# Top-32 attention, gate and phase mixer on one core: the threshold of each tile from one MAX8 with eight added columns

## The chip, the cores and the metric

The kernel runs on one core of a Trainium2 chip. The metric is device time in microseconds, the median of the runs taken; lower is better. Engines are named as in the profile: PE is TensorE (matmuls; PEld its weight loads), DVE is VectorE, ACT is ScalarE, POOL is GpSimd, SP is the queue that issues most DMAs.

## What is computed

Three stages in float32, for 4 batches, 8 heads, 576 tokens, 64 columns a head:

```python
scores = (q @ k.T) / sqrt(64)
kth = the 32nd largest score of each row
scores = where(scores >= kth, scores, -1e9)
attn = exp(scores - max); attn = attn / (sum(attn) + 1e-9)
x = attn @ v
gate = sigmoid(sum over 5 taps of conv_w[k] * x[t + k - 4])
x = (gate * (x @ w_val)) @ w_out
theta = x @ w_theta
u = x + w_tok_r @ (x * cos(theta)) + w_tok_i @ (x * sin(theta))
out = u + max(u @ w_ch, 0)
```

The change touches the second line alone, the search for the 32nd largest score of a row, and the scale in which the scores are kept for it.

## The kernel before

The 4 x 8 x 576 rows of scores are cut into 144 tiles of 128 rows and 576 columns. A loop over steps runs all engines through a software pipeline: in step i, tile i gets its first search and older tiles get their later stages. What a step does, and in which order, stands in a list of names (`STEP`, and `SOON` for the first half of the tiles). The instructions of VectorE and ScalarE stand in exactly that order; TensorE, GpSimd and the DMA queues are ordered by the scheduler by priority, which follows the order of the program.

What happens to tile i, with the lines:

- `scores_pe`, `scores_out` (L536, L550): TensorE makes the scores in PSUM, ScalarE copies them to SBUF with the factor 0.125 as tile `s`.
- `pick` (L565), step i: VectorE takes MAX8 (the eight largest, sorted) of each of six stretches of 96 columns, 48 candidates. Interleaved with this, the candidates of tile i - 1 are sorted by three MAX8 and two MATCH_REPLACE8: the 24 largest of them, `tops`.
- `count` (L581): ScalarE takes the sign of (24th candidate - score), +1 for scores below, -1 for the others, as `n`, and sums the signs in `acc`. A row with c scores not below has acc = 576 - 2c.
- `below` (L589), step i + 2: GpSimd makes y = s * n. Scores below keep their value, those above turn negative. Tile y has one buffer, so the next y waits for `rest`.
- `rest` (L596), step i + 3: VectorE takes MAX8 of y, the eight largest scores below the 24th candidate.
- `nmax` (L603): GpSimd negates the largest and the 24th of three tiles, for the exponent's bias and for the check.
- `select` (L605), once for a group of three tiles: c is 24 if the candidates held all of the 24 largest, and more if a stretch had over eight of them. Three VectorE operations pick the (32 - c)th of the eight: compare `counts` with `acc` (L611), multiply with the eight (L613), sum over eight (L614). They go into the list `apart`, from which `mask_between` (L1247) takes one at a time, three in a step: one ahead of the mask and two behind it. The operations of the list `fill` (the conversion of weights, L328, L329, L324, up to 300 us) are taken in the same places.
- `expo` (L645): ScalarE takes exp(s - max).
- `mask` (L650), step i + 6: VectorE makes (s >= threshold) * exp and its sum in one operation (L656).
- `turn`, `close`: TensorE transposes the masked tile and multiplies by v; VectorE, ScalarE and GpSimd divide by the sums (L700, L701, L767) and make the gate (L792 to L804).

The dense stages (`front`, `back`) are cut into pieces that TensorE does between the steps; the last of them follow after the tiles. `check` (L631) runs once behind the last tile: if a threshold is not above a tiny bound, or a 24th candidate isn't positive, a flag makes the whole program run again in a safe form (`safe`), which searches directly.

Of the kernel before, what the change touches and what calls it, by code (L numbers as in the profile page):

```python
# [11 lines left out]
F32 = mybir.dt.float32  # L12
# [4 lines left out]
AF = mybir.ActivationFunctionType  # L17
ALU = mybir.AluOpType
# [58 lines left out]
@with_exitstack  # L77
def attention_gate_phase_mixer(ctx, tc, *tensors):


    nc = tc.nc
    keep = ctx.enter_context(tc.tile_pool(name="keep", bufs=1))
    flag = keep.tile([1, 1], F32, name="flag")
    mixer(tc, *tensors, flag)

    over = nc.values_load(flag.bitcast(I32), min_val=0, max_val=0x7F000000,
                          skip_runtime_bounds_check_because="a count of rows")
    with tc.If(over > 0):
        mixer(tc, *tensors, None)
# [3 lines left out]
def mixer(ctx, tc, qT, kT, vt, w_val, conv_t, w_out, w_theta, w_tok, w_ch, out, flag):  # L93
    nc = tc.nc
    safe = flag is None
    P = 128
    B, S, DM = vt.shape
# [5 lines left out]
    G = 3  # L103
    NSUB = 6
    SUB = S // NSUB
    K = 32
    KC = 24
# [3 lines left out]
    CUT = 2 * P  # L111
    COLS = ((0, CUT), (CUT, S))
    LAG = G + FLAG

    cp = ctx.enter_context(tc.tile_pool(name="cp", bufs=1))
    io = ctx.enter_context(tc.tile_pool(name="io", bufs=1))
    sp = ctx.enter_context(tc.tile_pool(name="sp", bufs=1))
    wk = ctx.enter_context(tc.tile_pool(name="wk", bufs=1))
# [34 lines left out]
    N = len(seq)  # L153
# [10 lines left out]
    make_identity(nc, ident)  # L164
    ones = cp.tile([P, 1], F32, name="ones")
    nc.gpsimd.memset(ones, 1.0)
    counts = cp.tile([P, G, K - KC], F32, name="counts")
    for i in range(K - KC):
        nc.gpsimd.memset(counts[:, :, i : i + 1], S - 2.0 * (K - 1 - i))
    trig_bias = cp.tile([P, 1], F32, name="trig_bias")  # L170
    nc.gpsimd.memset(trig_bias[:64], math.pi / 2)
    nc.gpsimd.memset(trig_bias[64:], 0.0)
# [3 lines left out]
    nc.gpsimd.memset(magic, MAGIC)  # L176

    awake = cp.tile([P, 1], F32, name="awake")
    said = cp.tile([1, 2], F32, name="said")
    thrs = cp.tile([P, N], F32, name="thrs")  # L180
    least = cp.tile([P, N, 2], F32, name="least")
    taken, lacking = set(), {}
    raws, heads, there, ready = {}, {}, set(), set()
    s_tiles, s_psum, groups, xT, gate, W, ms = {}, {}, {}, {}, {}, {}, {}
    owed = [0.0]
    jobs, later, mid, extras, chains, flowing, fill, apart = [], [], [], [], [], [], [], []

    evicted = [None]
    last = {}

    def tabled(out, src, func, **more):

        ins = nc.scalar.activation(out, src, func, **more).ins  # L193
        table = func == AF.Sin
        if (not table) in last and TABLED:
            tc.add_manual_dep(ins, last[not table].name, mybir.DependencyInfo(
                mybir.DependencyClass.NoSync, mybir.DependencyReason.DATA), reason="one table at a time")
        last[table] = ins

    def run(fs):  # L200
        for f in fs:
            f()
# [342 lines left out]
    def scores_out(i):  # L545
        banks = s_psum.pop(i)
        if i < N:
            st = sp.tile([P, S], F32, tag="s", name=f"s_{i}", bufs=LAG + TO + AHEAD)
            for (lo, hi), (bank, _) in zip(COLS, banks):
                evicted[0] = nc.scalar.activation(st[:, lo:hi], bank[:, : hi - lo], AF.Copy, scale=0.125).ins  # L550
            s_tiles[i] = st
        for _, follow in banks:
            run(follow)

    def group(i):
        g, k = divmod(i, G)
        if g not in groups:
            d = {}
            for nm, shape in (("cand", [P, G, 8 * NSUB]), ("tops", [P, G, K]), ("acc", [P, G]),
                              ("eq", [P, G, K - KC])):  # L560
                d[nm] = wk.tile(shape, F32, tag=nm, name=f"{nm}_{g}", bufs=2 if nm == "cand" else 3)
            groups[g] = d
        return groups[g], k
# [25 lines left out]
    def below(i):  # L589

        d, k = group(i)
        y = wk.tile([P, S], F32, tag="y", name=f"y_{i}")
        nc.gpsimd.tensor_tensor(y, s_tiles[i], d.pop(("n", k)), ALU.mult)  # L593
        d["y", k] = y

    def rest(i):  # L596
        d, k = group(i)
        nc.vector.max(d["tops"][:, k, KC:K], d.pop(("y", k)))  # L598

    def nmax(g):  # L600

        d = groups[g]
        nc.gpsimd.tensor_scalar(least[:, g * G : g * G + G, :], d["tops"][:, :, 0 : KC : KC - 1], -1.0, None, ALU.mult)  # L603

    def select(g):  # L605

        if safe:
            return one_by_one(g)
        d = groups[g]
        tops, acc = d["tops"], d["acc"]  # L610
        apart.append(lambda: nc.vector.tensor_tensor(  # L611
            d["eq"], counts, acc.unsqueeze(2).broadcast_to([P, G, K - KC]), ALU.is_equal))
        apart.append(lambda: nc.vector.tensor_tensor(d["eq"], d["eq"], tops[:, :, KC:], ALU.mult))  # L613
        apart.append(lambda: nc.vector.tensor_reduce(thrs[:, g * G : g * G + G], d["eq"], mybir.AxisListType.X, ALU.add))  # L614

    def one_by_one(g):

        d = groups[g]
        spare = wk.tile([P, S], F32, tag="ct", name=f"spare_{g}")
        for k in range(G):  # L620
            src = s_tiles[g * G + k]
            for r in range(K // 8):
                top = d["tops"][:, k, 8 * r : 8 * r + 8]
                nc.vector.max(top, src)
                if r < K // 8 - 1:
                    nc.vector.match_replace(spare, top, src, LOWEST)
                    src = spare
            nc.vector.tensor_copy(thrs[:, g * G + k : g * G + k + 1], d["tops"][:, k, K - 1 : K])
        nmax(g)

    def check():  # L631

        bad = cp.tile([P, 2], F32, name="bad")
        worse = wk.tile([P, S], F32, tag="ct", name="worse")[:, :N]
        nc.vector.tensor_scalar(worse, thrs, 2.0 ** -100, None, ALU.is_le)
        nc.vector.tensor_reduce(bad[:, 0:1], worse, mybir.AxisListType.X, ALU.add)
        nc.vector.tensor_scalar(worse, least[:, :, 1], -2.0 ** -100, None, ALU.is_ge)
        nc.vector.tensor_reduce(bad[:, 1:2], worse, mybir.AxisListType.X, ALU.add)

        def on_pe(spare):  # L640
            nc.tensor.matmul(spare[:1, :2], ones, bad, start=True, stop=True)
            return lambda: nc.scalar.activation(said, spare[:1, :2], AF.Copy, accum_out=flag)
        extras.append((2, on_pe))

    def expo(i):  # L645
        e = seq[i]
        e.exp = wk.tile([P, S], F32, tag="e", name=f"e_{i}", bufs=2)
        tabled(e.exp, s_tiles[i], AF.Exp, bias=least[:, i, 0:1], scale=1.0)

    def mask(i):  # L650
        e = seq[i]
        part = e.part
        if e is part["tiles"][0]:
            part["sums"] = wk.tile([P, 5], F32, tag="sums", name=f"sums_{e.u}_{e.x}", bufs=3)
        p = s_tiles[i]
        nc.vector.scalar_tensor_tensor(p, p, thrs[:, i : i + 1], e.exp, ALU.is_ge, ALU.mult,  # L656
                                       accum_out=part["sums"][:, e.slot : e.slot + 1])

    def turn(i):
# [389 lines left out]
    def fine_tok(w):  # L1049

        both = []
        for k in range(2):
            n = 2 * w + k
            if n < LAG + TO + AHEAD:
                both.append(sp.tile([P, S], F32R, tag="s", name=f"tok_{w}_{k}", bufs=LAG + TO + AHEAD))
            else:
                tag = ("kh0", "kh1", "kl0", "kl1", "kh", "kl", "qh", "ql")[n - LAG - TO - AHEAD]
                both.append(io.tile([P, S], F32R, tag=tag, name=f"tok_{w}_{k}"))
# [104 lines left out]
    def end(u, x):  # L1163
        return parts[u, x]["tiles"][-1].i + LAG + TO

    stages = []
    for b in range(B):
        late = b == B - 1
        f = 1.275 if b in THREE else 1.675
# [26 lines left out]
    def work(ns, rest=0.0, more=MORE):  # L1196
        p = tc.cur_priority
        tc.cur_priority = p + LOW_BY
        work_(ns, rest, more)
        tc.cur_priority -= LOW_BY  # L1200
# [18 lines left out]
    for k, part in enumerate(order):  # L1219
# [7 lines left out]
        elif split or x == 0:  # L1227
            when = (i0 - 7, i0 - 5, i0 - 5, i0 - 4, i0 - 3) if split else (i0 - 9, i0 - 8, i0 - 7, i0 - 6, i0 - 3)
            a = (u, x if split else None)
            for step, do in zip(when, (load_heads, split_high, split_low, *(  # L1230
                    lambda u, x, j=j: double(u, j, x) for j in range(2)))):
# [5 lines left out]
    for i in range(AHEAD):  # L1237
        scores_pe(i)
        if i < AHEAD - 1:
            scores_out(i)  # L1240
# [6 lines left out]
    def mask_between(i):  # L1247

        for x in range(3):
            for fs in (fill, apart):  # L1250
                if fs:
                    fs.pop(0)()
            if x == 0:
                inside(i, mask)

# [10 lines left out]
    def inside(i, f):  # L1266
        if 0 <= i < N:
            f(i)
# [18 lines left out]
    def by_group(i, f):  # L1287
        if i % G == 0:
            inside(i, lambda i: f(i // G))
# [4 lines left out]
    def work_1(i):  # L1294
# [3 lines left out]
    DO = {  # L1298
        "count": lambda i: None if safe else inside(i - 1, count),
        "expo": lambda i: inside(i - LAG + 1, expo),  # L1300
        "select": lambda i: by_group(i - G - 2, select),
        "nmax": lambda i: None if safe else by_group(i - G - 1, nmax),
        "check": lambda i: None if safe or i != N + G else check(),
        "mask": lambda i: mask_between(i - LAG),
# [72 lines left out]
```

## Time and profile before

| | |
|---|---|
| median of 3 runs | 872.44 us (871.95 to 874.28) |
| the profiled execution | 878.3 us, span 876.5 us |
| TensorE busy | 757.3 us (86%) |
| VectorE busy | 725.9 us (83%) |
| ScalarE busy | 652.3 us (74%) |
| GpSimd busy | 409.2 us (47%) |

The span runs from the first to the last instruction that the profiler recorded. Shares are means over the whole span. The 144 tiles are done at some 741 us; the last dense stages follow. A row of a group gives an engine's operations of one line and shape, their number, the busy time, the mean of one, and the idle time of the engine just ahead of them with what ended it. Records of successive VectorE operations overlap a little, so the sum of records is more than the time they take.

### The profile page before, as it was taken

The numbers are of one execution on the slowest core, as the hardware profiler recorded it, in microseconds if no ns is written. First come the engines' busy times: TensorE is split into PE (matmuls) and PEld (weight loads), VectorE is DVE, ScalarE is ACT, GpSimd is POOL, SyncE is SP. The second block draws the span as 40 slices with busy tenths as digits, with TensorE's granted clock in tenths as the row PEclk, the third lists the DMA queues.
The fourth block names the chain that finished last, engine by engine and source line by source line (L and its number), as shares of the span: only waits on it lengthen the run. The fifth ranks groups of instructions, "written<-read, shape, count | busy, mean of one in ns | idle before, by whom it ended". The sixth has DMA issues, their size and how long they took to land.

```text
span 876.5 us, 15920 instructions
## 1 busy us (share of the span) xinstructions
PE 757.3 (86%) x4526; PEld 575.6 (66%) x4526; DVE 725.9 (83%) x2952; ACT 652.3 (74%) x1591; POOL 409.2 (47%) x435
## 2 busy tenths in 40 slices
PE   4477876947879689989798999999998999999995
PEld 2344554624556358676678577769697776699895
DVE  5999998879999778989999999899988697444522
ACT  5787896878979587687878898798987895445611
POOL 4655555344555324354758634445677233003700
PEclk9996788966899979999899999999999999999998
DMA  5665555613433124324735552132755110042001
GB/s 148 169 183 166 143 141 152 174 48 92 131 92 93 43 67 128 94 55 114 225 112 185 191 163 61 46 94 58 216 135 154 44 67 15 1 155 93 3 1 58
DMA packets 73601, 94.35 MB, mean 108 GB/s; under 512 B 13728, under 2 KB 37152, under 8 KB 73504
## 3 DMA queue, kind: packets, MB, share of 16 engines
q1 hardware_dynamic: 73184, 92.82, 37.6%
q8 instruction: 38, 0.62, 0.3%
q14 instruction: 59, 0.48, 0.2%
q10 hardware_dynamic: 320, 0.43, 0.1%
HBM read 49.96 MB, written 13.11 MB: 72 GB/s over the span
## 4 chain that ended last, share of the span: by engine, by line
PE 41%; DVE 37%; ACT 11%; issue 5%; DMA 2%; POOL 2%; SPq 1%; ACTq 0%; POOLq 0%; DVEq 0%
PE py L1090 8%; DVE cand L573 8%; PE px L749 8%; DVE tops L598 6%; DVE s L656 5%; PE ph L507 4%; PE pval L507 3%; DVE cand L579 3%; PE pt L669 3%; PE py L1109 3%; DVE tops L577 3%; PE px2t L507 3%; DVE gp L804 3%; PE ps L536 2%; PE pth L507 2%
## 5 line engine op out<-in xcount | busy, mean ns | idle before, releaser
L593 POOL TENSOR_TENSOR y<-s,n 128x576 f32<-128x576 f32 x144 | 188.4, 1308 | 199.5 <-DVE tops L598 101.6
L573 DVE MAX8 cand<-s 128x8 f32<-128x96 f32 x864 | 210.8, 245 | 1.4 <-ACT s L550 1.4
L585 ACT ACTIVATE n<-s,tops 128x576 bf16<-128x576 f32 x144 | 112.0, 778 | 50.3 <-DVE tops L577 34.4
L656 DVE SCALAR_TENSOR_TENSOR s<-s,thrs,e 128x576 f32<-128x576 f32 x144 | 137.9, 958 | 5.7 <-ACT e L193 5.7
L669 PE MATMUL pt<-ident,s 128*128 128x128 f32 x576 | 99.0, 296 | 49.3 <-ACT pT L688 34.5
L550 ACT ACTIVATE s<-ps 128x256 f32<-128x256 f32 (+1 forms) x288 | 103.9, 406 | 38.2 <-PE ps L722 15.0
L669 PEld LDWEIGHTS pt<-ident,s 128*128 128x128 f32 x576 | 71.1, 149 | 78.1 <-ACT pT L688 42.6
L1090 PE MATMUL py<-w_tok,z 128*128 128x256 f32 (+1 forms) x432 | 115.6, 410 | 6.9 <-DVE z L949 6.7
L749 PE MATMUL px<-pT,v 128*64 128x256 f32 (+3 forms) x640 | 113.3, 455 | 8.2 <-ACT pT L688 7.2
L598 DVE MAX8 tops<-y 128x8 f32<-128x576 f32 x144 | 108.0, 750 | 11.7 <-POOL y L593 11.7
L193 ACT ACTIVATE e<-s,least 128x576 f32<-128x576 f32 x144 | 110.5, 768 | 1.3 <-DVE s L656 0.9
L536 PE MATMUL ps<-kh_None,q 128*128 128x256 f32 x240 | 96.9, 410 | 5.9 <-ACT rb L729 2.7
L688 ACT COPY pT<-pt 128x512 f32<-128x512 f32 x128 | 73.2, 571 | 29.1 <-PE px L749 14.7
L1090 PEld LDWEIGHTS py<-w_tok,z 128*128 128x128 f32 x432 | 78.4, 191 | 24.8 <-issue 7.3
L749 PEld LDWEIGHTS px<-pT,v 128*64 128x64 f32 (+1 forms) x640 | 46.1, 148 | 58.8 <-issue 30.9
L577 DVE MAX8 tops<-cand 128x8 f32<-128x48 f32 x432 | 82.9, 192 | 0.1
L537 PE MATMUL ps<-kl_None,q 128*128 128x256 f32 x240 | 73.7, 309 | 0.0
L536 PEld LDWEIGHTS ps<-kh_None,q 128*128 128x128 f32 x240 | 48.5, 202 | 26.9 <-ACT s L550 7.5
L536 PE MATMUL ps<-kh,q 128*128 128x256 f32 (+1 forms) x80 | 40.1, 506 | 20.5 <-ACT s L550 11.4
L579 DVE MATCH_REPLACE8 cand<-tops,cand 128x48 f32<-128x48 f32 x288 | 55.3, 192 | 0.0
L804 DVE SCALAR_TENSOR_TENSOR gp<-xT,w_conv,gp 128x576 f32<-128x576 f32 (+2 forms) x60 | 50.1, 836 | 4.7 <-POOL gp L796 4.0
L537 PEld LDWEIGHTS ps<-kl_None,q 128*128 128x128 f32 x240 | 49.1, 205 | 3.4 <-issue 1.6
(208 smaller groups left out, 1695.7 us busy)
## 6 DMA issues: line engine op xcount, KB each, us to landing
kh_None<-kh_None SPq DMA_DIRECT2D x48, 144.0 KB, 2.5
kl_None<-kl_None SPq DMA_DIRECT2D x48, 144.0 KB, 2.6
v<-in_vt_dram SPq DMA_DIRECT2D x20, 256.0 KB, 2.9
out_dram<-x2T SPq DMA_DIRECT2D x16, 256.0 KB, 3.2
w<-ch SPq DMA_DIRECT2D x16, 256.0 KB, 4.3
w<-theta SPq DMA_DIRECT2D x16, 256.0 KB, 5.5
raw_hi<-in_w_tok_dram SPq DMA_DIRECT2D x14, 256.0 KB, 2.9
kh<-kh SPq DMA_DIRECT2D x24, 144.0 KB, 2.4
```

The lines of the kernel that those rows point to most:

```text
L193: ins = nc.scalar.activation(out, src, func, **more).ins
L536: nc.tensor.matmul(bank[:, :w], q2, kh[:, lo:hi], start=(j == js[0]), stop=False)
L537: nc.tensor.matmul(bank[:, :w], q2, kl[:, lo:hi], start=False, stop=(j == js[-1]))
L573: nc.vector.max(d["cand"][:, k, 8 * x : 8 * x + 8], s_tiles[i][:, x * SUB : (x + 1) * SUB])
L577: nc.vector.max(top, c)
L585: nc.scalar.activation(n, s_tiles[i], AF.Sign, bias=d["tops"][:, k, KC - 1 : KC], scale=-(1.0 + 2.0 ** -22), accum_out=d["acc"][:, k : k + 1])
L593: nc.gpsimd.tensor_tensor(y, s_tiles[i], d.pop(("n", k)), ALU.mult)
L598: nc.vector.max(d["tops"][:, k, KC:K], d.pop(("y", k)))
L656: nc.vector.scalar_tensor_tensor(p, p, thrs[:, i : i + 1], e.exp, ALU.is_ge, ALU.mult, accum_out=part["sums"][:, e.slot : e.slot + 1])
L669: nc.tensor.transpose(e.pt[:, c, :], p[:, c * P : (c + 1) * P], ident)
L749: nc.tensor.matmul(px[64 * j : 64 * j + 64, :], v[r, c, 64 * j : 64 * j + 64], pT[r, k, :], start=(c == 0), stop=(c == NF), skip_group_che ...
L1090: nc.tensor.matmul(ps, z[:, m * P : (m + 1) * P], W["tok"][:, w, lo:hi], start=(i + k == 0), stop=(i == NF))
```

## The change

The threshold now comes out of `rest` itself. Tile y gets eight more columns: GpSimd writes steps[j] - acc there, which is 2(c - 24 - j) - 1, in a second instruction behind y. For a row with c scores not below the 24th candidate, c - 24 of them are 1 or more and the others negative. The scores are kept times 2^-30, so that every score is far below 1. MAX8 over the 584 columns then has those c - 24 columns first and the next scores behind them, and its eighth value is the 32nd largest score. MAX8 writes its eight values into `thrs` so that the eighth of each tile stays: tile i writes one column to the left of tile i - 1 and overwrites only what is no longer needed. The three operations of `select`, the list `apart`, and the tiles `eq` and `counts` go away; `select` is left for the safe form alone. The exponent and the bias are scaled back by 2^30, and `check` has a third test (a threshold of 0.5 or more).

```diff
+    NK = K - KC
+    SMALL = 1.0 if safe else 2.0 ** -30
...
-    counts = cp.tile([P, G, K - KC], F32, name="counts")
-    for i in range(K - KC):
-        nc.gpsimd.memset(counts[:, :, i : i + 1], S - 2.0 * (K - 1 - i))
+    steps = cp.tile([P, NK], F32, name="steps")
+    for i in range(NK):
+        nc.gpsimd.memset(steps[:, i : i + 1], S - 2.0 * (KC + i) - 1.0)
...
-    thrs = cp.tile([P, N], F32, name="thrs")
+    thrs = cp.tile([P, N + NK - 1], F32, name="thrs")
...
-                evicted[0] = nc.scalar.activation(st[:, lo:hi], bank[:, : hi - lo], AF.Copy, scale=0.125).ins
+                evicted[0] = nc.scalar.activation(st[:, lo:hi], bank[:, : hi - lo], AF.Copy, scale=0.125 * SMALL).ins
...
-        y = wk.tile([P, S], F32, tag="y", name=f"y_{i}")
-        nc.gpsimd.tensor_tensor(y, s_tiles[i], d.pop(("n", k)), ALU.mult)
+        y = wk.tile([P, S + NK], F32, tag="y", name=f"y_{i}")
+        nc.gpsimd.tensor_tensor(y[:, :S], s_tiles[i], d.pop(("n", k)), ALU.mult)
+        nc.gpsimd.tensor_tensor(y[:, S:], steps, d["acc"][:, k : k + 1].broadcast_to([P, NK]), ALU.subtract)
         d["y", k] = y
 
     def rest(i):
         d, k = group(i)
-        nc.vector.max(d["tops"][:, k, KC:K], d.pop(("y", k)))
+        nc.vector.max(thrs[:, N - 1 - i : N - 1 - i + NK], d.pop(("y", k)))
+
+    def thr(i):
+        at = N - 1 - i + NK - 1
+        return thrs[:, at : at + 1]
...
-        nc.gpsimd.tensor_scalar(least[:, g * G : g * G + G, :], d["tops"][:, :, 0 : KC : KC - 1], -1.0, None, ALU.mult)
+        nc.gpsimd.tensor_scalar(least[:, g * G : g * G + G, :], d["tops"][:, :, 0 : KC : KC - 1], -1.0 / SMALL, None,
+                                ALU.mult)
-
-    def select(g):
-
-        if safe:
-            return one_by_one(g)
-        d = groups[g]
-        tops, acc = d["tops"], d["acc"]
-        apart.append(lambda: nc.vector.tensor_tensor(
-            d["eq"], counts, acc.unsqueeze(2).broadcast_to([P, G, K - KC]), ALU.is_equal))
-        apart.append(lambda: nc.vector.tensor_tensor(d["eq"], d["eq"], tops[:, :, KC:], ALU.mult))
-        apart.append(lambda: nc.vector.tensor_reduce(thrs[:, g * G : g * G + G], d["eq"], mybir.AxisListType.X, ALU.add))
...
-        nc.vector.tensor_scalar(worse, thrs, 2.0 ** -100, None, ALU.is_le)
-        nc.vector.tensor_reduce(bad[:, 0:1], worse, mybir.AxisListType.X, ALU.add)
-        nc.vector.tensor_scalar(worse, least[:, :, 1], -2.0 ** -100, None, ALU.is_ge)
-        nc.vector.tensor_reduce(bad[:, 1:2], worse, mybir.AxisListType.X, ALU.add)
+        for j, (what, limit, op) in enumerate(((thrs[:, NK - 1 :], 2.0 ** -90, ALU.is_le),
+                                               (thrs[:, NK - 1 :], 0.5, ALU.is_ge),
+                                               (least[:, :, 1], -2.0 ** -60, ALU.is_ge))):
+            nc.vector.tensor_scalar(worse, what, limit, None, op)
+            nc.vector.tensor_reduce(bad[:, j : j + 1], worse, mybir.AxisListType.X, ALU.add)
...
-        tabled(e.exp, s_tiles[i], AF.Exp, bias=least[:, i, 0:1], scale=1.0)
+        tabled(e.exp, s_tiles[i], AF.Exp, bias=least[:, i, 0:1], scale=1.0 / SMALL)
...
-        nc.vector.scalar_tensor_tensor(p, p, thrs[:, i : i + 1], e.exp, ALU.is_ge, ALU.mult,
+        nc.vector.scalar_tensor_tensor(p, p, thr(i), e.exp, ALU.is_ge, ALU.mult,
                                        accum_out=part["sums"][:, e.slot : e.slot + 1])
...
-            for fs in (fill, apart):
-                if fs:
-                    fs.pop(0)()
+            if fill:
+                fill.pop(0)()
...
-        "select": lambda i: by_group(i - G - 2, select),
+        "select": lambda i: by_group(i - G - 2, one_by_one) if safe else None,
```

## Rows read from the trace of the kernel before

**Rows 1.** Busy time by stretch: window, length, busy us (instructions) of each engine

```profile
20.00:300.00 280.00, 212.12 (x1014) 135.88 (x1015) 260.30 (x1155) 226.31 (x597) 148.77 (x171) 0.85 0.47 127
300.00:741.00 441.00, 410.94 (x2621) 320.80 (x2621) 401.75 (x1641) 362.92 (x862) 223.82 (x209) 0.97 0.39 110
741.00:876.50 135.50, 125.45 (x870) 113.04 (x868) 54.32 (x107) 52.18 (x108) 28.07 (x22) 0.97 0.16 50
sum 876.50, PE 757.33 PEld 575.57 DVE 725.86 ACT 652.34 POOL 409.18; mean PE 189.33 PEld 143.89 DVE 181.46 ACT 163.08 POOL 102.29
```

**Rows 2.** Chain that ended last: whole span; by line, 300 to 741 us

```profile
PE 41%; DVE 37%; ACT 11%; issue 5%; DMA 2%; POOL 2%; SPq 1%; ACTq 0%; POOLq 0%; DVEq 0%
...
by line: PE py L1090 13.7%; PE px L749 10.1%; DVE s L656 8.2%; DVE cand L573 7.4%; DVE tops L598 5.5%; PE pt L669 4.8%; DVE gp L804 3.8%; PE ps L536 3.6%; PE pval L507 3.5%; DVE cand L579 2.8%; DVE tops L577 2.7%; PE ps L537 2.6%; PE pth L5
```

**Rows 3.** VectorE groups by form: count | busy us, mean ns | idle

```profile
L573 DVE MAX8 cand<-s 128x8 f32<-128x96 f32 x864 | 210.8, 245 | 1.4 <-ACT s L550 1.4
L656 DVE SCALAR_TENSOR_TENSOR s<-s,thrs,e 128x576 f32<-128x576 f32 x144 | 137.9, 958 | 5.7 <-ACT e L193 5.7
L598 DVE MAX8 tops<-y 128x8 f32<-128x576 f32 x144 | 108.0, 750 | 11.7 <-POOL y L593 11.7
...
L613 DVE TENSOR_TENSOR eq<-eq,tops 128x24 f32<-128x24 f32 x48 | 16.9, 353 | 0.0
L611 DVE TENSOR_TENSOR eq<-counts,acc 128x24 f32<-128x24 f32 x48 | 16.9, 351 | 0.0
...
L614 DVE TENSOR_REDUCE thrs<-eq 128x3 f32<-128x24 f32 x48 | 8.4, 176 | 1.0
```

**Rows 4.** Timeline at 304 us, GpSimd then VectorE, around a group's selection

```profile
304.60 0.23 POOL L700 TENSOR_SCALAR rs<-sums 128x5 f32<-128x5 f32 x1 [1.20 <-DVE eq L613]
...
303.53 0.17 DVE L611 TENSOR_TENSOR eq<-counts,acc 128x24 f32<-128x24 f32 x1
303.62 0.81 DVE L656 SCALAR_TENSOR_TENSOR s<-s,thrs,e 128x576 f32<-128x576 f32 x1
...
304.35 0.18 DVE L613 TENSOR_TENSOR eq<-eq,tops 128x24 f32<-128x24 f32 x1
304.57 0.18 DVE L614 TENSOR_REDUCE thrs<-eq 128x3 f32<-128x24 f32 x1
304.66 0.81 DVE L804 SCALAR_TENSOR_TENSOR gp<-xT,w_conv,gp 128x576 f32<-128x576 f32 x1
```

**Rows 5.** Timeline at 243.6 us on VectorE, in the first part

```profile
243.59 0.17 DVE L613 TENSOR_TENSOR eq<-eq,tops 128x24 f32<-128x24 f32 x1
243.70 0.43 DVE L324 SCALAR_TENSOR_TENSOR raw_hi<-raw_hi,tmp 128x256 int32<-128x256 int32 x1
```

**Rows 6.** Timeline at 424 us, GpSimd then VectorE: start us, length us

```profile
423.97 1.27 POOL L593 TENSOR_TENSOR y<-s,n 128x576 f32<-128x576 f32 x1
425.20 1.40 POOL L244 TENSOR_TENSOR ql_None<-ql_None,qh_None 128x576 fp32r<-128x576 f32 x1
...
424.19 1.10 DVE L611 TENSOR_TENSOR eq<-counts,acc 128x24 f32<-128x24 f32 x1
425.21 2.01 DVE L656 SCALAR_TENSOR_TENSOR s<-s,thrs,e 128x576 f32<-128x576 f32 x1
```

**Rows 7.** GpSimd: smallest two-input form by group; line 603, ns min/median/max

```profile
L342 POOL TENSOR_TENSOR w_conv<-raw_hi 128x20 int32<-128x20 int32 x1 | 0.2, 218 | 0.8 <-DVE raw_hi L324 0.8
...
L603 POOL TENSOR_SCALAR least<-tops x48: 233/742/892, 19.4 to 734.1; 128x6 f32<-128x6 f32 x48
```

**Rows 8.** Timeline at 307 us, GpSimd then VectorE

```profile
306.29 1.27 POOL L593 TENSOR_TENSOR y<-s,n 128x576 f32<-128x576 f32 x1 [1.46 <-DVE tops L598]
307.71 0.89 POOL L603 TENSOR_SCALAR least<-tops 128x6 f32<-128x6 f32 x1
...
307.70 0.81 DVE L656 SCALAR_TENSOR_TENSOR s<-s,thrs,e 128x576 f32<-128x576 f32 x1
```

**Rows 9.** Waits of VectorE: us in total, times, longest us

```profile
DVE tops L598 <- POOL y L593: 11.7, 9, 2.4
```

More of the change, by code (lines that the diff above doesn't have):

```diff
@@ L178, in mixer @@
     awake = cp.tile([P, 1], F32, name="awake")
-    said = cp.tile([1, 2], F32, name="said")
-    thrs = cp.tile([P, N], F32, name="thrs")
+    said = cp.tile([1, 3], F32, name="said")
+    thrs = cp.tile([P, N + NK - 1], F32, name="thrs")
     least = cp.tile([P, N, 2], F32, name="least")
@@ L185, in mixer @@
     owed = [0.0]
-    jobs, later, mid, extras, chains, flowing, fill, apart = [], [], [], [], [], [], [], []
+    jobs, later, mid, extras, chains, flowing, fill = [], [], [], [], [], [], []
     evicted = [None]
@@ L558, in group @@
             d = {}
-            for nm, shape in (("cand", [P, G, 8 * NSUB]), ("tops", [P, G, K]), ("acc", [P, G]),
-                              ("eq", [P, G, K - KC])):
+            for nm, shape in (("cand", [P, G, 8 * NSUB]), ("tops", [P, G, K if safe else KC]), ("acc", [P, G])):
                 d[nm] = wk.tile(shape, F32, tag=nm, name=f"{nm}_{g}", bufs=2 if nm == "cand" else 3)
@@ L627, in one_by_one @@
                     src = spare
-            nc.vector.tensor_copy(thrs[:, g * G + k : g * G + k + 1], d["tops"][:, k, K - 1 : K])
+            nc.vector.tensor_copy(thr(g * G + k), d["tops"][:, k, K - 1 : K])
         nmax(g)
     def check():
-        bad = cp.tile([P, 2], F32, name="bad")
+        bad = cp.tile([P, 3], F32, name="bad")
         worse = wk.tile([P, S], F32, tag="ct", name="worse")[:, :N]
-        nc.vector.tensor_scalar(worse, thrs, 2.0 ** -100, None, ALU.is_le)
-        nc.vector.tensor_reduce(bad[:, 0:1], worse, mybir.AxisListType.X, ALU.add)
-        nc.vector.tensor_scalar(worse, least[:, :, 1], -2.0 ** -100, None, ALU.is_ge)
-        nc.vector.tensor_reduce(bad[:, 1:2], worse, mybir.AxisListType.X, ALU.add)
+        for j, (what, limit, op) in enumerate(((thrs[:, NK - 1 :], 2.0 ** -90, ALU.is_le),
[3 more added lines that the diff above has]
+            nc.vector.tensor_reduce(bad[:, j : j + 1], worse, mybir.AxisListType.X, ALU.add)
         def on_pe(spare):
-            nc.tensor.matmul(spare[:1, :2], ones, bad, start=True, stop=True)
-            return lambda: nc.scalar.activation(said, spare[:1, :2], AF.Copy, accum_out=flag)
-        extras.append((2, on_pe))
+            nc.tensor.matmul(spare[:1, :3], ones, bad, start=True, stop=True)
+            return lambda: nc.scalar.activation(said, spare[:1, :3], AF.Copy, accum_out=flag)
+        extras.append((3, on_pe))
     def expo(i):
```

## The prediction, made before the changed kernel was run

> **What bounds the kernel now.** I read the busy time by stretch first. From 20 to 300 us VectorE is busy 260.3 of 280 us and TensorE 212.1; from 300 to 741 us, where the attention tiles end, VectorE has 401.8 of 441 us and TensorE 410.9 [rows 1]. So VectorE leads the first part and stands level with TensorE in the second; GpSimd has 409.2 us in the whole span, 47% of it. The chain that ended last says the same: 37% of the span is VectorE's and 41% TensorE's [rows 2]. In the last 135 us TensorE has 125.5 and VectorE 54.3 [rows 1], and VectorE hardly appears there in the chain, so VectorE's 37% (324 us) lie within the first 741 us, a share of 0.44 there. That is the rate at which I let VectorE time turn into time of the end.
>
> The groups by line and form then show what VectorE does per tile: six MAX8 over 96 columns, the sort of the candidates, one MAX8 over y (576 columns, L598), the mask (L656), and per group of three tiles the three small operations that the change removes, L611, L613 and L614, with 16.9, 16.9 and 8.4 us in 48 groups [rows 3]. The means of L611 and L613, 351 and 353 ns, are not their plain price: the timeline has both at 0.17 to 0.18 us where nothing is in their way [rows 4, 5]. It also shows what stretches them: at 424.19 us L611 stands for 1.10 us, until GpSimd's running operation ends, and the mask behind it for 2.01 us in place of 0.81, behind the next GpSimd operation that starts at 425.20 [rows 6]. Element-wise VectorE operations with two inputs in SBUF and GpSimd's operations take turns; the MAX8 rows do not lengthen in this way.
>
> **What is removed.** A record overlaps the next by some 0.08 us, so I price an operation from its start to the next one's start. In the second part L611 takes 303.53 to 303.62 us, 0.09; L613 takes 304.35 to 304.57, 0.22, because L614 waits for its output; L614 takes 304.57 to 304.66, 0.09 [rows 4]. That is 0.40 us per group. In the first part the conversion of weights stands between them and L613 is followed after 0.11 us [rows 5], which makes 0.29. L611 runs 18 times before 300 us and 30 times after: 18 x 0.29 + 30 x 0.40 = 17.2 us.
>
> The blocked time comes on top: 48 x (351 - 170) = 8.7 us at L611 and 48 x (353 - 175) = 8.5 us at L613. It is not simply saved, since the next two-input operation inherits the block. Behind L611 comes always the mask, which would wait for the same end: I count nothing of the 8.7. But where L611 used up the turn between two GpSimd operations, the mask now gets it and saves 2.01 - 0.81 = 1.2 us [rows 6]; such masks of about 2.0 us I found four times, 4.8 us, and I take half, 2.4, because a new GpSimd operation also takes a turn there. Behind L613 comes L614, a reduction that is never long, and then often an operation that reads PSUM: I take half of 8.5, 4.2 us. The bounds for the blocked part are nothing and 17.2 + 4.8 us. VectorE loses 17.2 + 2.4 + 4.2 = 23.8 us.
>
> **What is added on VectorE.** MAX8 goes from 245 ns for 96 columns to 750 for 576, 1.05 ns a column [rows 3]; eight more columns in 144 tiles make 1.2 us. The check gets two more operations once, after the last tile, where TensorE sets the end: nothing, and half a microsecond if that cover were gone.
>
> **What is added on GpSimd.** 144 products of eight columns, each behind its y, in the queue ahead of the splits, the weight conversion and the negated maxima. The trace has none of this kind. The nearest row is the two-input operation over 20 columns, 218 ns [rows 7]; the far one is the six-column operation of L603, 233 ns at the least, 742 at the median, 892 at most [rows 7]. I take 0.22, since L603 is long only where it meets the mask: at 307.71 us it begins 0.01 us after the mask and lasts 0.89 [rows 8]. Busy time on GpSimd grows by 144 x 0.22 = 32 us to 441, half the span (144 x 0.74 = 107 us, or 59%, at the far end); what is queued behind it comes 0.2 us later, under idle time of that engine. Below nothing it cannot come, for it is an operation more.
>
> What matters is when y is ready for MAX8, and whether the operation holds up VectorE. In the ordinary step y ends at 306.29 + 1.27 = 307.56 us, and the mask begins at 307.70 [rows 8]. Two GpSimd operations with no wait between them follow at once (y of 423.97 us ends as the split begins at 425.20 [rows 6]), so the new one begins some 0.13 us ahead of the mask and goes first. MAX8 over y comes only behind the mask, 0.8 us later or more: hidden. It is not hidden in three sorts of tiles. In nine tiles MAX8 already waits for y, 11.7 us in all [rows 9]: 9 x 0.22 = 2.0 us. In some 25 tiles y runs late and a mask is blocked behind it (144 x (958 - 810) = 21.3 us of blocking, near 0.9 each [rows 3, 4]); there the mask goes first and the new operation after it. If MAX8 follows that mask directly, say in ten, it waits 0.2 us more: 2.0. In all 25 the next two-input operation may lose 0.1 us: 2.5. Together 6.5 us; none and 144 x 0.22 = 32 us are the bounds.
>
> How long the small operation keeps VectorE out is the open price. L700 on GpSimd runs from 304.60 to 304.83 us, and L804, with two SBUF inputs, begins at 304.66 and takes 0.81 us, no longer than the mask of the same 576 columns [rows 4]: it was not held up by the 0.17 us that were left. The Trainium skill (SBUF — State Buffer, Who interferes with whom) states that the shared port pair is held for the whole instruction and the other engine fully blocks; the long L611 and L603 agree, this L804 doesn't. By that rule the time would be that of the rival "port" below, some 878 us, in place of 866.
>
> **The sum.** -23.8 + 1.2 + 6.5 = -16.1 us of VectorE time. At 0.44 that is 7.1 us; since VectorE's share falls as it gets shorter, and TensorE has only 30 us idle in the second part, I take 0.40: 6.4 us. The profiled execution would go from 876.5 to 870.1 us of span. It stood at 878.3 us, 0.7% over the median of 872.4; I take the 6.4 us off the median unscaled: **866.0 us**. The factor 2^-30, the compare and the exponent's scale change numbers alone, no operation: nothing. No DMA is added or moved.
>
> **Rivals.** *Port* (slower): each of the 144 small operations holds the port for its whole record just as VectorE wants it, since the two stand only 0.13 us apart. It decides once it costs VectorE more than (23.8 - 1.2) / 144 = 0.16 us a tile. At 0.22 it costs 32 us in place of 6.5: -23.8 + 1.2 + 32 = +9.4, and with the delayed MAX8 of the 19 tiles (4.0) +13.4; at 0.44, 5.9 us slower: 878. L603's long records speak for it, L804 beside L700 against it. The Trainium skill (Perfetto Trace Analysis, Optimizing Scalar/DVE Operations) warns that moving work between these two engines may not help, because they share a port; no row here shows this for eight columns. *TensorE absorbs it* (no change): in the second part TensorE is busy 93% and VectorE's gain becomes its wait. Only the first part pays: 18 x 0.29 = 5.2, less about 1.2 of costs, at 0.44: 1.8 us, 870.6. Against it, the six VectorE lines named in the chain of the second part hold 30% of it by themselves [rows 2]. *No inheritance* (more): the removed records, 42.2 us less 144 x 0.08 of overlap = 30.7, go whole and additions cost only 3: 27.7 x 0.5 = 14 us, 858. *It doesn't do what it says*: if the check counted a row, the second, safe pass would run and the time nearly double, to some 1,740 us. Scaling by a power of two is exact, so nothing speaks for it but its possibility.
>
> **How the numbers follow.** Forecast 0.50, TensorE absorbs 0.22, port 0.13, no inheritance 0.13, second pass 0.02. A measurement tells 0.3%, 2.6 us, from no change. Faster by more: nine tenths of the forecast, all of no inheritance, a fifth of the absorbed case, 0.45 + 0.13 + 0.05 = 0.63; slower 0.15; the rest 0.22. The range runs from 858, no inheritance, to 876, which takes in the absorbed case and half of what the port might cost; port and second pass (0.15) and a little at the lower end stay outside.
>
> **What would show it.** L611, L613 and L614 are gone; MAX8 over y near 758 ns; new GpSimd records near 0.22 us, with a second heap near 0.8 where they meet a mask; the wait of MAX8 for y near 14 to 16 us in place of 11.7; the mask's mean near 950 ns; VectorE's busy time some 30 us less (records overlap). Wrong would be: a mask mean well above 958 (port), or a VectorE shorter by 20 us with its waits for TensorE longer by as much (absorbed).

## The result and the profile after

| | before | changed | ratio, 95% interval |
|---|---|---|---|
| median | 873.29 us (4 runs) | 863.37 us (861.84 to 865.15, 4 runs) | 0.9888 [0.9863, 0.9913] |
| measured again later | 871.98 us (9 runs) | 864.82 us (5 runs) | 0.9914 [0.9900, 0.9927] |
| span of the profiled execution | 876.5 us | 861.4 us | |

The change makes the kernel 0.9 to 1.1% faster, 7 to 10 us. The profiled pair differs by 15.1 us because the profiled execution of before was a long one (878.3 us against a median of 873). Every run of the changed kernel (865.59 us or less) is shorter than every run of the kernel before (870.96 us or more). TensorE's granted clock, a mean over the span, does not order the times: runs of the kernel before took 871.24 us at 0.920 of full speed and 877.66 us at 0.932, and those of the changed kernel have 0.927 to 0.940. The page of the changed kernel, busy time of each engine and the chain that ended last:

```profile
PE 749.4 (87%) x4526; PEld 572.4 (66%) x4526; DVE 700.8 (81%) x2810; ACT 650.2 (75%) x1591; POOL 448.1 (52%) x579
...
PE 44%; DVE 28%; ACT 13%; issue 5%; POOL 4%; DMA 3%; SPq 1%; ACTq 0%; POOLq 0%; DVEq 0%
```

VectorE has 25.1 us less to do (725.9 before), GpSimd 38.9 us more. TensorE's busy time is 7.9 us less for the same 4526 matmuls. This is no second cause: the kernels with three products and with three reductions (below), which differ in three operations of VectorE alone, are 7.0 us apart in it. In the chain VectorE falls from 37 to 28%, and the other engines have more [rows 2]. The busy time of the second part of the changed kernel, whose tiles end near 727 us (window, length, busy us of PE, PEld, DVE, ACT, POOL):

```profile
300.00:727.00 427.00, 402.73 (x2604) 316.23 (x2601) 378.79 (x1544) 360.51 (x861) 249.12 (x296) 0.98 0.41 114
```

This answers to the second row of [rows 1]. The second part became 14 us shorter and VectorE lost 23 us there. It was the less busy of the two leading engines there already, with 402 us against TensorE's 411, and is further behind now, 379 against 403. VectorE's mask and its MAX8 over y, and the new GpSimd operation:

```profile
L653 DVE SCALAR_TENSOR_TENSOR s<-s,thrs,e 128x576 f32<-128x576 f32 x144 | 143.8, 999 | 5.3 <-ACT e L195 5.3
L600 DVE MAX8 thrs<-y 128x8 f32<-128x584 f32 x144 | 109.3, 759 | 17.4 <-POOL y L595 17.2
```

```profile
L595 POOL TENSOR_TENSOR y<-steps,acc 128x8 f32<-128x8 f32 x144 | 44.9, 312 | 0.0
```

MAX8 takes 759 ns with eight columns more, 750 before [rows 3]. The mask's mean is up from 958 to 999 ns: part of what blocked the removed operations now blocks the mask. MAX8 waits 17.4 us for y where it waited 11.7 [rows 9]. The new operation has 202 ns at the median and 312 in the mean. The timeline of an ordinary step shows why it does no harm (GpSimd, then VectorE):

```profile
302.97 1.27 POOL L594 TENSOR_TENSOR y<-s,n 128x576 f32<-128x576 f32 x1 [0.74 <-DVE thrs L600]
304.20 0.20 POOL L595 TENSOR_TENSOR y<-steps,acc 128x8 f32<-128x8 f32 x1
```

```profile
304.39 0.80 DVE L653 SCALAR_TENSOR_TENSOR s<-s,thrs,e 128x576 f32<-128x576 f32 x1
```

The new operation begins 0.04 us before the record of y ends, and is done 0.01 us after the mask begins; the mask takes its plain 0.80 us. In the whole trace 47 masks begin while the record of the new operation still runs, with up to 0.15 us of it left, and 46 of them take 0.81 us or less.

### The profile page after: what moved, and what is told of

It reads as the page before. It is cut to its first block, busy times and chain, and to the rows that moved or that the text cites. A ratio compares the mean times of both kernels' runs of the same rounds, so it can differ in the third digit from the quotient of the medians.

```text
span 861.4 us, 15930 instructions
## 1 busy us (share of the span) xinstructions
PE 749.4 (87%) x4526; PEld 572.4 (66%) x4526; DVE 700.8 (81%) x2810; ACT 650.2 (75%) x1591; POOL 448.1 (52%) x579
## 4 chain that ended last, share of the span: by engine, by line
PE 44%; DVE 28%; ACT 13%; issue 5%; POOL 4%; DMA 3%; SPq 1%; ACTq 0%; POOLq 0%; DVEq 0%
PE py L1087 10%; PE px L746 8%; DVE cand L574 6%; DVE thrs L600 5%; PE ph L509 5%; DVE s L653 3%; PE pt L666 3%; PE py L1106 3%; PE ps L538 3%; PE pval L509 3%; PE px2t L509 3%; DVE gp L801 3%; PE pth L509 2%; DVE cand L580 2%; DVE tops L578 2%
## 5 line engine op out<-in xcount | busy, mean ns | idle before, releaser
L653 DVE SCALAR_TENSOR_TENSOR s<-s,thrs,e 128x576 f32<-128x576 f32 x144 | 143.8, 999 | 5.3 <-ACT e L195 5.3
L600 DVE MAX8 thrs<-y 128x8 f32<-128x584 f32 x144 | 109.3, 759 | 17.4 <-POOL y L595 17.2
L746 PE MATMUL px<-pT,v 128*64 128x256 f32 (+3 forms) x640 | 107.1, 433 | 8.9 <-ACT pT L685 8.1
L746 PEld LDWEIGHTS px<-pT,v 128*64 128x64 f32 (+1 forms) x640 | 43.3, 140 | 57.1 <-issue 26.1
L801 DVE SCALAR_TENSOR_TENSOR gp<-xT,w_conv,gp 128x576 f32<-128x576 f32 (+2 forms) x60 | 47.6, 793 | 4.8 <-POOL gp L793 4.1
```

Of the source, the lines that this page charges most:

```text
L600: nc.vector.max(thrs[:, N - 1 - i : N - 1 - i + NK], d.pop(("y", k)))
L653: nc.vector.scalar_tensor_tensor(p, p, thr(i), e.exp, ALU.is_ge, ALU.mult, accum_out=part["sums"][:, e.slot : e.slot + 1])
L746: nc.tensor.matmul(px[64 * j : 64 * j + 64, :], v[r, c, 64 * j : 64 * j + 64], pT[r, k, :], start=(c == 0), stop=(c == NF), skip_group_che ...
```

## The experiments

All ratios are to the kernel before, run beside each kernel on the same chip. Differences to the changed kernel are taken from its two medians, 863.37 and 864.82 us, often from another chip. The kernel before has medians from 871.98 to 874.03 us in these comparisons, so a difference of under 2 us to the changed kernel says nothing. Two theories stood against each other: what the removed operations cost was their own plain time, or it was the time that they stood blocked by GpSimd; and the added GpSimd operation was hidden, or paid by VectorE.

**The added operation alone, on the kernel before.**

```diff
+    steps = cp.tile([P, NK], F32, name="steps")
+    for i in range(NK):
+        nc.gpsimd.memset(steps[:, i : i + 1], -2.0 * S - i)
...
+        nc.gpsimd.tensor_tensor(y[:, S:], steps, d["acc"][:, k : k + 1].broadcast_to([P, NK]), ALU.subtract)
```

> The kernel before with the GpSimd operation of eight columns added behind y and MAX8 over 584 columns; the columns hold values far below every score, so the selection by the three VectorE operations stays as it is. Theory 'mostly hidden' (the new operation runs under the MAX8 stretch and costs only in the tiles where y is late): 2 to 5 us slower than before, ratio 1.002 to 1.006. Rival 'port' (it holds VectorE up in every tile): 8 us slower or more, ratio over 1.009. Rival 'free': ratio within 0.002 of 1.

873.75 us, ratio 1.0004 [0.9987, 1.0022], which is 1.1 us faster to 1.9 us slower: free. 144 operations on GpSimd and eight more columns of MAX8 cost nothing that can be measured here, and 'port' is refuted.

**The removal alone.**

```diff
-        nc.gpsimd.tensor_tensor(y[:, S:], steps, d["acc"][:, k : k + 1].broadcast_to([P, NK]), ALU.subtract)
...
-        nc.vector.max(thrs[:, N - 1 - i : N - 1 - i + NK], d.pop(("y", k)))
+        nc.vector.max(thrs[:, N - 1 - i : N - 1 - i + NK], d.pop(("y", k))[:, :S])
```

> The changed kernel without the GpSimd operation and with MAX8 over 576 columns; it leaves out the correction for rows whose candidates missed one of the 24 largest, so their threshold is one place too low. It shows what the removal of the three VectorE operations brings by itself. 'Mostly hidden': 2 to 5 us below the changed kernel, some 859 to 861 us where that has 863, and the mask's mean falls back to 950 ns or less. 'Port': some 853 us or below, mask mean near 920. 'Free': as the changed kernel, mask mean near 1000.

864.79 us, ratio 0.9903 [0.9880, 0.9925]: the same as the changed kernel. So the whole gain is the removal's, and 'free' is right by the time, though not in its detail: the mask's mean is 959 ns, not near 1000. Part of the difference turns up at L800, whose 36 operations over 576 columns have a mean of 1006 ns, against 933 at the same line (L801) of the changed kernel. VectorE's groups here:

```profile
L652 DVE SCALAR_TENSOR_TENSOR s<-s,thrs,e 128x576 f32<-128x576 f32 x144 | 138.2, 959 | 5.8 <-ACT e L195 5.8
L599 DVE MAX8 thrs<-y 128x8 f32<-128x576 f32 x144 | 108.0, 750 | 15.7 <-POOL y L594 15.7
```

MAX8 waits 15.7 us for y without any operation behind y. Most of the longer wait in the changed kernel (17.4 us, 11.7 before) is thus not the new operation's; that VectorE, with less to do, comes to MAX8 sooner would explain it.

**The added operation twice.**

```diff
         nc.gpsimd.tensor_tensor(y[:, S:], steps, d["acc"][:, k : k + 1].broadcast_to([P, NK]), ALU.subtract)
+        nc.gpsimd.tensor_tensor(y[:, S:], steps, d["acc"][:, k : k + 1].broadcast_to([P, NK]), ALU.subtract)
```

> The changed kernel with the operation of eight columns issued twice in a row. 'Mostly hidden': the second one starts some 0.05 us ahead of the mask in the ordinary step and so begins to get in its way, and MAX8 waits 0.2 us longer where it waits for y: 2 to 6 us slower than the changed kernel. 'Port': as much again as the first one cost, 8 us or more. 'Free': no change.

867.86 us, ratio 0.9939 [0.9918, 0.9960]: 3 to 4.5 us over the changed kernel's two medians, and each of its 8 runs (866.38 us or more) is above all 9 of the changed kernel (865.59 us or less). The first operation is free, a second is not. VectorE's groups show MAX8 waiting for it:

```profile
L601 DVE MAX8 thrs<-y 128x8 f32<-128x584 f32 x144 | 109.6, 761 | 26.4 <-POOL y L596 25.4
```

That is 9.0 us more idle time ahead of MAX8 than with one. The mask's mean fell meanwhile to 934 ns, so it was the wait for y, not the port.

**Three operations put back, with the port and without it.** In both kernels three operations of 24 columns per group stand where the selection stood, and nothing uses them; those of the first kernel have two inputs in SBUF, those of the second have one. The lines that set up their inputs and their places are left out here.

```diff
+        for _ in range(3):
+            apart.append(lambda: nc.vector.tensor_tensor(extra[0], counts, counts, ALU.mult))
```

> The changed kernel with three products of 24 columns (two inputs in SBUF) per group of three tiles put back in the places that the selection had; nothing uses them. 'Blocked time': 48 x 3 operations with the port, plain 48 x 0.3 = 14 us, blocked as L611 and L613 were: 8 to 13 us slower than the changed kernel, at or above the kernel before. 'Plain time alone' (blocks are inherited by the next operation anyway): 4 to 6 us slower, the same as with three reductions.

```diff
+        for _ in range(3):
+            apart.append(lambda: nc.vector.tensor_reduce(extra[1], counts, mybir.AxisListType.X, ALU.add))
```

> As before with three reductions of 24 columns (one input) in the same places, which L614 showed to be never long. Plain 48 x 0.3 = 14 us of VectorE at 0.35: 4 to 6 us slower than the changed kernel by both theories. 'Blocked time': at least 4 us faster than with three products. 'Plain time alone': within 2 us of it.

The products: 874.99 us, ratio 1.0000 [0.9984, 1.0016], the whole gain is gone. The reductions: 868.01 us, ratio 0.9923 [0.9897, 0.9950]. The order of instructions on every other engine is the same in the two. Their operations by duration (ns min/median/max, first and last start), products first:

```profile
L619 DVE TENSOR_TENSOR extra<-counts x144: 151/177/1400, 24.8 to 741.0; 128x24 f32<-128x24 f32 x144
```

```profile
L619 DVE TENSOR_REDUCE extra<-counts x144: 151/170/179, 25.0 to 732.0; 128x3 f32<-128x24 f32 x144
```

And the busy time of each engine in the two pages, products first:

```profile
PE 758.4 (87%) x4526; PEld 577.7 (66%) x4526; DVE 729.1 (83%) x2954; ACT 653.0 (75%) x1591; POOL 444.8 (51%) x580
```

```profile
PE 751.4 (87%) x4526; PEld 572.2 (66%) x4526; DVE 713.6 (82%) x2954; ACT 651.7 (75%) x1591; POOL 446.0 (51%) x580
```

The plain durations are alike, 177 and 170 ns; the products reach 1400 ns, no reduction exceeds 179. The products hold VectorE 15.5 us longer, nearly all of it blocked, and that costs 7.0 us at the end; the plain time, 713.6 - 700.8 = 12.8 us, costs 3 to 5 us. 'Blocked time' holds. The Trainium skill (SBUF — State Buffer, Who interferes with whom) states that a VectorE instruction with two SBUF inputs contends with a GpSimd instruction that reads SBUF, and that a reduction never does on this chip; the two rows of durations agree.

**The eight columns written by VectorE.**

```diff
+        nc.vector.tensor_scalar(y[:, S:], steps, d["acc"][:, k : k + 1], None, ALU.subtract)
```

> The changed kernel with the eight columns written by VectorE, directly ahead of its MAX8, in place of by GpSimd. The plain price is one VectorE operation of some 0.1 us and a wait of MAX8 for it, 0.2 us in all as with L613 and L614: 144 x 0.2 = 29 us of VectorE, about what the removal freed. 'VectorE time sets the pace at some 0.35 of it': 8 to 12 us slower than the changed kernel, near the kernel before. 'It was the port that the removed operations paid with': only 2 to 5 us slower, since this operation stands in the MAX8 stretch.

892.91 us, ratio 1.0211 [1.0183, 1.0239]: 28 to 30 us slower than the changed kernel, beyond both expectations. The timeline, and then the line's durations (ns min/median/max), show two reasons:

```profile
265.92 0.23 DVE L600 TENSOR_SCALAR y<-steps,acc 128x8 f32<-128x8 f32 x1
266.25 0.77 DVE L601 MAX8 thrs<-y 128x8 f32<-128x584 f32 x1
```

```profile
L600 DVE TENSOR_SCALAR y<-steps,acc x144: 187/225/1535, 13.6 to 754.1; 128x8 f32<-128x8 f32 x144
```

From its start to that of MAX8, which waits for its output, pass 0.33 us, not 0.2: 144 x 0.33 = 48 us. And it too is blocked, up to 1.5 us: its mean of 349 ns is 124 over the median, 18 us in all. Against these 66 us the mask is blocked less, with a mean of 927 ns in place of 999, 10 us in all. So VectorE has some 55 us more to get through, and they cost some 29 at the end. Moving eight columns from VectorE to GpSimd is worth that much.

**The eight columns ahead of the product.**

```diff
-        nc.gpsimd.tensor_tensor(y[:, :S], s_tiles[i], d.pop(("n", k)), ALU.mult)
         nc.gpsimd.tensor_tensor(y[:, S:], steps, d["acc"][:, k : k + 1].broadcast_to([P, NK]), ALU.subtract)
+        nc.gpsimd.tensor_tensor(y[:, :S], s_tiles[i], d.pop(("n", k)), ALU.mult)
```

> The changed kernel with the eight columns written ahead of the product y in place of behind it. GpSimd's work is the same, but y now ends some 0.2 us later, 0.07 us after the mask's usual start, and where the mask is blocked by y, y no longer has an operation behind it that needs another turn. If the margin of 0.13 us in the ordinary step matters more: 1 to 5 us slower than the changed kernel, mask mean over 1040 ns. If the extra turn in late steps matters more: 1 to 4 us faster, the wait of MAX8 for y back near 12 us.

869.55 us, ratio 0.9958 [0.9941, 0.9974]: 5 to 6 us slower than the changed kernel, as the margin theory had it in the time, but not for its reason. The mask's mean is 972 ns, below the changed kernel's 999, where over 1040 was expected. An ordinary step (GpSimd, then VectorE):

```profile
304.76 1.27 POOL L595 TENSOR_TENSOR y<-s,n 128x576 f32<-128x576 f32 x1
```

```profile
306.01 0.80 DVE L653 SCALAR_TENSOR_TENSOR s<-s,thrs,e 128x576 f32<-128x576 f32 x1
```

y ends at 306.03 us by its record, the mask begins at 306.01 and takes its plain time: y is not in its way. VectorE has no more to do than in the changed kernel (701.8 us busy, 700.8 there), and MAX8 waits 18.9 us for y, against 17.2 there. The product begins 0.2 us later, so the one buffer of the signs is held 0.2 us longer too; but with two buffers for the signs nothing is gained (below). What carries the 5 to 6 us stays open.

**Two buffers for y.**

```diff
-        y = wk.tile([P, S + NK], F32, tag="y", name=f"y_{i}")
+        y = wk.tile([P, S + NK], F32, tag="y", name=f"y_{i}", bufs=2)
```

> The changed kernel with two buffers for y in place of one, so that a product need not wait for the MAX8 of the tile before. 'Margin' (what the order of the two GpSimd operations cost is y ending too late against the mask): y begins earlier where the signs are ready and the margin grows: 2 to 6 us faster than the changed kernel. 'Alignment' (the one buffer is what keeps y in the MAX8 stretch): y now begins at any time and meets the two-input operations of VectorE more often, blocked time over median well above 50 us: 3 us slower or more.

884.52 us, ratio 1.0122 [1.0104, 1.0140]: about 20 us slower than the changed kernel, 'alignment'. y now waits almost only for the signs and starts in the midst of VectorE's two-input operations. Its group on GpSimd, the timeline (GpSimd, then VectorE), and VectorE's group of the line that it meets:

```profile
L594 POOL TENSOR_TENSOR y<-s,n 128x576 f32<-128x576 f32 x144 | 196.2, 1362 | 206.9 <-ACT n L586 198.2 <-DVE tops L578 2.7 <-DMA raw_lo<-in_w_ch_dram 2.5
```

```profile
304.67 1.39 POOL L594 TENSOR_TENSOR y<-s,n 128x576 f32<-128x576 f32 x1 [0.60 <-ACT n L586]
```

```profile
304.95 1.39 DVE L326 SCALAR_TENSOR_TENSOR raw_lo<-raw_lo,tmp 128x256 int32<-128x256 int32 x1
```

```profile
L326 DVE SCALAR_TENSOR_TENSOR raw_hi<-raw_hi,tmp 128x256 int32<-128x256 int32 x34 | 26.6, 782 | 1.2
```

That line has 782 ns in the mean, where its plain time is 0.43 us [rows 5]. VectorE's busy time is 722.9 us, 22 more than in the changed kernel, and some 20 of them are this line's, with both of its tiles. The order of operations is that of the changed kernel on every engine except GpSimd. What looked like a missing buffer is what keeps y beside the MAX8 operations, which did not lengthen: over y they took 718 to 771 ns here, 726 to 773 in the changed kernel.

**Two buffers for the signs, and a sum of its own for each tile.**

```diff
-        n = wk.tile([P, S], BF16, tag="n", name=f"n_{i}")
+        n = wk.tile([P, S], BF16, tag="n", name=f"n_{i}", bufs=2)
```

> The changed kernel with two buffers for the signs n. ScalarE waits 25 us in all for the operation of eight columns before it writes the next n, 10.6 us for y before the change. If that wait costs time: 2 to 5 us faster. If ScalarE's waits are covered: within 1.5 us, with the wait gone.

```diff
+        acc = wk.tile([P, 1], F32, tag="acc1", name=f"acc_{i}", bufs=4)
...
-                             accum_out=d["acc"][:, k : k + 1])
+                             accum_out=acc)
```

> The changed kernel with two buffers for n and a tile of its own for each tile's sum of signs, where three tiles share one before. With two n alone ScalarE still waited 28 us for the operation of eight columns. If that wait comes from the shared tile of sums, it is gone here; if it holds up the chain, the time falls by 2 to 5 us against the changed kernel; if it is covered, it stays within 1.5 us, or rises, as with two y, should the signs and then y move out of the MAX8 stretch.

The second kernel has both. 865.77 us, ratio 0.9902 [0.9886, 0.9919], and 864.52 us, ratio 0.9918 [0.9905, 0.9932]: no change in either. By the list of waits ScalarE still waits 28.5 us and 30.3 us for the operation of eight columns before it writes the signs. The timeline of such a wait with two buffers for the signs shows that this is a misreading (VectorE, GpSimd, ScalarE):

```profile
338.89 0.19 DVE L578 MAX8 tops<-cand 128x8 f32<-128x48 f32 x1
```

```profile
338.98 0.20 POOL L595 TENSOR_TENSOR y<-steps,acc 128x8 f32<-128x8 f32 x1
```

```profile
339.17 0.78 ACT L586 ACTIVATE n<-s,tops 128x576 bf16<-128x576 f32 x1 [1.52 <-POOL y L595]
```

The signs begin before the eight columns are done, and 0.09 us after the MAX8 that gives them the 24th candidate. In all of these waits, here and in the changed kernel, they begin 0.09 to 0.12 us after that MAX8. They wait for VectorE, as in the kernel before (34.4 us, 30 times); the operation of eight columns only ends at about the same time. ScalarE's wait for the product, 12.7 us in the changed kernel and due to the buffer of the signs, is gone in both kernels, and the time did not fall: it was covered.

Two buffers for y together with two for the signs gave no time: with them a pool of 45 KB a partition no longer fits in SBUF, where 44.6 are left.

**The changed kernel again, and without the scale.**

> The changed kernel itself, on the same chip as the run beside it: ratio to the kernel before between 0.986 and 0.991, as measured first.

```diff
-    SMALL = 1.0 if safe else 2.0 ** -30
+    SMALL = 1.0
```

> The changed kernel with the scores kept unscaled (the factor 2^-30 set to 1; the added columns are odd whole numbers and the scores of this input stay below 1). The same instructions with other numbers: within 1.5 us of the changed kernel. More would mean that the values of the data, or the layout of the program, move the time by as much as the effects looked for here.

The first gave the second row of the table at the top, 0.9914. Its ratio stands just above the expected 0.991, so ratios here repeat to some 0.3%. The second: 862.67 us, ratio 0.9862 [0.9835, 0.9889], 0.7 and 2.2 us below the changed kernel's two medians. The second difference is above the 1.5 us expected, but the changed kernel's own two medians differ by 1.5 us. A cost of the scale is not shown, and a small one is not excluded.

## Why the prediction was right, and where it was not

866.0 us were forecast, 863.4 to 864.8 measured; faster by 6.4 us, measured 7 to 10. The direction, the range and what bounds the kernel were right. Two terms of the sum were mis-sized, both on the same side: the blocked time that goes was put too small, and the added work too large.

- **What bounds the kernel.** Right for this change: by VectorE's busy time 9.9 / 25.1 = 0.39 of it (0.29 by the second measurement) came off the end, and 7.0 / 15.5 = 0.45 for the blocked products; 0.40 was taken. It is no constant of the kernel: the eight columns on VectorE cost some 29 us for 41 us more busy time (741.8 us), 0.7, and two buffers for y some 20 for 22, 0.9. With two buffers for y the 61st mask already begins 20 us late, at 357 us, so the loss comes in where VectorE leads [rows 1]; that this makes the rate higher is argued, not shown.
- **Plain time removed, 17.2 us.** About right, or some 4 us too large. Three reductions in the same places are 12.8 us of VectorE's busy time; the sum counted L614's wait for L613 as well.
- **Blocked time removed, 6.6 us (2.4 + 4.2).** Too small. Putting products back brings 15.5 us of blocked time that reductions in the same places do not. With the plain 12.8 that is 28.3 us; the removal alone took 725.9 - 698.7 = 27.2 us off VectorE's busy time, and 23.8 were forecast, because the errors of the two terms partly cancel. The step that failed is "nothing of the 8.7", that the mask behind L611 inherits the block. It does so in part: its mean rose by 41 ns, 144 x 41 = 5.9 us, against the 17.2 us that L611 and L613 had stood blocked. With products put back the mask's mean is 927 ns, with reductions 982. The turn that the mask was to gain, 2.4 us, does not show in its mean. The rival 'no inheritance' was nearer to this, but its 858 us too low.
- **Added work, 7.7 us of VectorE time.** Too large: 0.0004 of the time in the first experiment, and by the second 700.8 - 698.7 = 2.1 us of busy time, of which MAX8 has 1.3, and 17.4 - 15.7 = 1.7 us of MAX8's wait, 3.8 in all. The 0.22 us for the operation was right (202 ns at the median), and so was its place ahead of the mask. The tiles where y is late cost less than forecast: MAX8's wait would have risen to 15.7 us anyway.
- **The sum.** -16.1 us of VectorE time was forecast, MAX8's longer wait for y counted in. In the same terms -25.1 us of busy time and 5.7 us more of that wait were measured, -19.4 us; at 0.40 that makes 7.8 us.
- **Port.** Refuted: the mask's mean did rise past 958, the sign named for it, but in the first experiment the operation costs nothing (mask 938 ns there), and 46 of the 47 masks that begin within its record keep their plain time. The row that spoke against this rival, L804 beside L700 [rows 4], was the right guide.
- **TensorE absorbs it.** Refuted in its main point, that only the first part pays: the 51st mask begins 3 us earlier than in the kernel before, at 279 us, and the last one 14 us earlier, at 736. VectorE's gain did become idle time in part, as the factor of 0.40 had it. Of 25.1 us less busy time 15.1 came off the profiled span, and only 7 to 10 by the medians; in the profiled pair VectorE's idle time grew by 10 us (876.5 - 725.9 = 150.6 us before, 861.4 - 700.8 = 160.6 after), of which 5.7 are MAX8's wait for y.
- **What was foretold for the profile.** MAX8 at 758 ns (759), its wait 14 to 16 us (17.4), VectorE 30 us less (25.1): close. The mask near 950 ns: wrong (999).

## What to carry to other kernels

Price a small VectorE operation with two SBUF inputs by its mean, not by its plain time, when GpSimd works beside it: the mean holds the blocked time, and much of that goes with it. Before a single buffer is doubled, look at what its wait keeps apart: here it held GpSimd's products in the stretch where VectorE runs operations that do not contend. A short GpSimd operation behind a long one was free here because it was all but over when the next contending VectorE operation began; a second one behind it was not, because MAX8 waited for it. And where a list of waits names an operation, check that the waiting one begins after its end.

## What the runs showed that was not expected

A VectorE operation is held up by less than what is left of the GpSimd record when it begins. The mask at 306.01 us, 0.02 ahead of y's recorded end, runs its plain 0.80 us, but a delay of 0.02 us could not be told from the spread. L804 lost nothing with 0.17 us of L700 left [rows 4]. A mask of the kernel before with far more left (GpSimd, then VectorE):

```profile
479.84 1.29 POOL L593 TENSOR_TENSOR y<-s,n 128x576 f32<-128x576 f32 x1
```

```profile
480.21 1.54 DVE L656 SCALAR_TENSOR_TENSOR s<-s,thrs,e 128x576 f32<-128x576 f32 x1
```

Of y 0.92 us are left, and the mask takes 0.73 us more than its plain 0.81, so 0.19 us of the record did not hold it up. The traces of all kernels agree: the masks that stood blocked behind one GpSimd operation lost what was left of it less some 0.19 us, the products of 24 columns what was left less some 0.13, and a mask with no more than 0.18 us left took its plain time unless the next GpSimd operation got in its way. The record of the eight columns lasts 0.20 us, so hardly any of it can block a mask. The Trainium skill (SBUF — State Buffer, Who interferes with whom) has the pair held for the whole instruction; by the records the hold looks shorter. Whether GpSimd lets go early, or VectorE needs the port only some time after its own record begins, is not shown.

And the eight columns that cost nothing on GpSimd cost some 29 us as one VectorE operation per tile.
